# Attention's weight tiles: the scale step on ScalarE, the sign step on GpSimd, two VectorE steps in place of three

## The chip, the cores and the metric

One core of a Trainium2 chip. The metric is device time in microseconds of one execution, as the median of the runs shown. One further execution was profiled; the trace is of that one. The engines are TensorE (PE), VectorE (DVE), ScalarE (ACT), GpSimd (POOL) and SyncE (SP, which here only issues DMAs).

## The reference

```
attention: B=4, H=8, S=576, D=64; scores = q k^T / 8 - slope_h * |i - j|, kept for 0 <= i - j < 128
           attn = softmax(scores); x = attn v, heads joined to d_model = 512
block 1:   x + relu(layer_norm(x) * g @ w_ch1) @ w_ch2                  (512 -> 2048 -> 512)
block 2:   h = relu(x @ w_in); h * sigmoid(conv3(h)) @ w_out            (512 -> 1024 -> 512)
```

All inputs and the output are 32-bit floats in the reference. The kernel is handed the weights as 64-bit floats, and it makes 32-bit ones of them itself: it views a weight as two 32-bit integers, a low word and a high word. The high word, read as a 32-bit float and multiplied by 2^-112, has its exponent moved to the right place; shifted left by three it makes room for the three top bits of the low word, which are or-ed in; the sign bit has to be put back.

## The kernel before, in words

**Attention** runs first. 72 query tiles of 128 positions (9 tiles for two batches, 4 pairs of heads, 2 such blocks) are taken in 18 groups of four, counted here from 0; group g has n = 4g, and its halves are a = n and b = n + 2. The loop (lines 859 to 916) is a software pipeline, and each engine works strictly in the order in which its instructions are written. In one pass, in this order: `scores` on TensorE (line 737); the last two exponentials of the former group on ScalarE (762); `copy_turned`, ScalarE's copies of transposed q and k (838), which the scores read; `copy_p` on ScalarE (789) and `select_p` on GpSimd (796) of an older half; `join` and `minima` on VectorE (748, 752); `shares` of the former half b, on VectorE and GpSimd (770 to 774); **`extras(n, 0)`**; `values` on TensorE (812); `exponentials(a)` on ScalarE, four instructions, and two of b; `shares(a)`; `turn_p`, `copy_p` and `select_p` of the former group's a; `turn_qk` on TensorE (711) for the next group; `copy_turned`; `turn_p` of the former b; issues of loads of q, k and v on SyncE; and **`extras(n, 1)`**. The buffers of raw q, k and v are few, so SyncE waits in them for TensorE.

**Weight tiles within attention.** Twelve of the 32 weight tiles of block 1 (512 KB raw each) are loaded and converted by `extras`, one step of `weights_step` at a time. A tile that starts at key s (FINE_START, all odd) has its load issued by SyncE in the second extras of group (s - 1)/2; its six stages (FINE, line 395) are taken at s + 3 to s + 8, where an even number is the first extras of a group and an odd one the second. So the stages are, in order: `rescale` on GpSimd (line 358), first extras of group (s + 3)/2; step 0 on VectorE (shift and mask, 373), second extras; step 1 (sign from the raw high word, 378), first extras; step 2 (bits of the low word, 383), second extras; `high` on ScalarE (412), first extras; `low` on VectorE (415), second extras. The keys are 1, 3, 5, 9, 11, 13, 17, 19, 21, 23, 25, 27: groups 2, 3, 4, 6, 7, 8, 10, 11, 12, 13, 14 and 15 begin one. The raw ring has three slots.

Other extras are a layer norm's statistics and subtraction (`LN_ATT`) and the convolution's weights (`small_inputs`, whose transpose on TensorE is line 695).

**Behind attention** all work is put into a plan (class Plan): each operation has an engine, an estimated duration, and its reads and writes. `schedule` plays it through, picks for each engine the operation with the earliest due time, and so sets the order in which instructions are written. Its clock starts at 0 with the first of these operations. DMAs count with a rate and a landing time, and may not start before `late`. In block 1 each of the other 20 tiles goes through `convert_next` (line 1223): load, signs on GpSimd (364), scale on ScalarE (356), two VectorE steps (1064, 383), ScalarE's high part (996) and GpSimd's subtraction for the low part (1236). Its raw tiles are two in `xnb` and three in `fa`; the last three of these are attention's as well. `mid` results lie in one PSUM bank or in the second part of `xnb`. TensorE's products (1035) then wait for these tiles; line 1011 on VectorE makes the low part of the hidden values.

Of the kernel before, what the change touches and what calls it, by code (L numbers as in the profile page):

```python
# [14 lines left out]
ALU = mybir.AluOpType  # L15
PSUM = bass.MemoryType.PSUM

P = 128
# [17 lines left out]
class Plan:  # L36
# [58 lines left out]
    def schedule(self, pe, goal, succ, cost, rate, landing, wait):  # L95
        ops = self.ops
        n = len(ops)
        horizon = max(goal.values()) + 1e5
        due = [0.0] * n
        for i in range(n - 1, -1, -1):  # L100
            if ops[i]["eng"] == "T":
                due[i] = goal[i]
            else:
                late = min((due[j] for j in succ[i]), default=horizon)
                due[i] = late - cost(ops[i]) - self.LAT
        left = [len(op["deps"]) for op in ops]
        ready = {}
        est = [op["late"] for op in ops]
        end = [0.0] * n
        free = {}  # L110
        lock = 0.0
        dma = 0.0
        pe_at = 0

        def put(i):
            ready.setdefault(ops[i]["eng"], []).append(i)

        for i in range(n):
            if not left[i]:
                put(i)  # L120
        order = []
        starts = [0.0] * n
        stall = []
        while len(order) < n:
            best = None
            for eng, items in ready.items():
                if not items:
                    continue
                if eng == "T":
                    i = pe[pe_at]  # L130
                    if left[i]:
                        continue
                    start = max(free.get(eng, 0.0), est[i])
                else:
                    at = {i: max(est[i], dma - 3000) if ops[i]["nbytes"] else est[i] for i in items}
                    when = max(free.get(eng, 0.0), min(at.values()))
                    soon = [i for i in items if at[i] <= when + wait]
                    i = min(soon, key=lambda i: (due[i], i))
                    if at[i] > when:
                        now = [j for j in items if at[j] <= when]  # L140
                        j = min(now, key=lambda j: (due[j], j))
                        if when + ops[j]["ns"] <= at[i] + wait or due[i] > when + ops[j]["ns"] + 1500:
                            i = j
                    start = max(when, at[i])
                if ops[i]["lock"]:
                    start = max(start, lock)
                if ops[i]["nbytes"]:
                    start = max(start, dma - 3000)
                if best is None or start < best[0]:
                    best = (start, eng, i)  # L150
            start, eng, i = best
            op = ops[i]
            ready[eng].remove(i)
            if eng == "T":
                if start > free.get(eng, 0.0) + 1:
                    stall.append((free.get(eng, 0.0), start, i))
                pe_at += 1
            free[eng] = start + op["ns"]
            end[i] = start + op["ns"]
            if op["lock"]:  # L160
                lock = end[i]
            if op["nbytes"]:
                dma = max(dma, start) + op["nbytes"] / rate / 1000
                end[i] = dma + landing
            order.append(i)
            starts[i] = start
            for j in succ[i]:
                est[j] = max(est[j], end[i] + (0 if ops[j]["eng"] == eng == "T" else self.LAT))
                left[j] -= 1
                if not left[j]:  # L170
                    put(j)
        self.due = due
        return order, stall, free, starts, max(starts[i] + ops[i]["ns"] for i in pe)
# [37 lines left out]
def tile_kernel(  # L211
# [28 lines left out]
    V, S, G, T = nc.vector, nc.scalar, nc.gpsimd, nc.tensor  # L240
# [87 lines left out]
    cvn = [0]  # L328
# [63 lines left out]

    FINE = (("rescale",), (0,), (1,), (2,), ("high",), ("low",))

    def weights_step(stages, start=True, only=None):

        now = [ld for ld in reversed(flight) if only in (None, ld["only"])]
        now = [(ld, ld["stages"].pop(0)) for ld in now]  # L400
        for j in range(max((len(do) for _, do in now), default=0)):
            for ld, do in now:
                if j >= len(do):
                    continue
                kind, i, raw = ld["kind"], ld["i"], ld["raw"]
                if do[j] == "rescale":
                    t = ld["t"] = fav(FA_CV0 + cvn[0] % 3 * 512, 512).bitcast(I32)
                    cvn[0] += 1
                    rescale(t, raw, G)
                elif do[j] == "high":  # L410
                    w = wtile(kind, i)
                    S.activation(w[:, 0, :], ld["t"].bitcast(F32), AF.Copy)
                elif do[j] == "low":
                    w = wtile(kind, i)
                    V.tensor_tensor(
                        out=w[:, 1, :], in0=ld["t"].bitcast(F32), in1=w[:, 0, :].bitcast(F32),
                        op=ALU.subtract,
                    )
                    flight.remove(ld)
                else:  # L420
                    to_f32(ld["t"], raw, (do[j],), ld["mid"])
        if todo and start:
            kind, i, pool = todo.pop(0)
            raw = scratch["raw"][:, scratch["n"] % 3, :]
            scratch["n"] += 1
            if kind in ("w1", "win"):
                src = (w_ch1 if kind == "w1" else w_in)[:, 2 * i * P : 2 * (i + 1) * P]
                nc.sync.dma_start(
                    raw.rearrange("p (c f) -> p c f", f=2 * P),
                    src.rearrange("(c p) f -> p c f", p=P),  # L430
                )
            else:
                src = (w_ch2 if kind == "w2" else w_out)[i * P : (i + 1) * P, :]
                nc.sync.dma_start(raw, src)
            flight.append({
                "kind": kind, "i": i, "pool": pool, "t": None, "mid": None, "only": only,
                "raw": raw.rearrange("p (n two) -> p n two", two=2), "stages": list(stages),
            })

# [97 lines left out]
    with ExitStack() as actx:  # L537
# [128 lines left out]
        for kind, r in ((1, 2), (3, 4)):  # L666
# [6 lines left out]
            op0=ALU.add, op1=ALU.add,  # L673
# [166 lines left out]

        def extras(n: int, m: int):
            for args in fine_at.get(n // 2 + m, ()):
                weights_step(FINE, *args)
            for u in (n + 2 * m, n + 2 * m + 1):
                if u in SMALL_AT:
                    small_inputs(SMALL_AT.index(u))
                for stage, j in LN_ATT.get(u, ()):
                    layer_norm(0, j, stage, ps_r, "ptr")
# [168 lines left out]
    def dma(dst, src, nbytes, late_at=0):  # L1017

        plan.add("SP", 70, lambda: nc.sync.dma_start(dst, src), [src], [dst], nbytes=nbytes, late=late_at)
# [22 lines left out]
        reads = [a for it in items for a in it]  # L1042
        plan.add("T", ns * len(items), go, reads, [out])

    BF0 = 2000

    def convert(kind: str, i: int, raw, cv, mid=None, eng="V"):

        late_at = BF0 if raw is None else 0
        src = {"w1": w_ch1, "win": w_in, "w2": w_ch2, "wout": w_out}[kind]  # L1050
        if kind in ("w1", "win"):
            dma(
                raw.rearrange("p (c f) -> p c f", f=2 * P),
                src[:, 2 * i * P : 2 * (i + 1) * P].rearrange("(c p) f -> p c f", p=P), 524288,
            )
        else:
            dma(raw, src[i * P : (i + 1) * P, :], 524288)
        rp = raw.rearrange("p (n two) -> p n two", two=2)
        if mid is not None:
            plan.add("G", 702, lambda: signs(cv, rp), [raw], [cv])  # L1060
# [162 lines left out]
    def convert_next():  # L1223

        kind, f, _ = todo.pop(0)
        n = conv_n[0]
        conv_n[0] += 1
        raw = RAWS[n % len(RAWS)]
        cv = fav(FA_CV0 + (cvn[0] + n) % NCV * 512, 512).bitcast(I32)
        convert(kind, f, raw, cv, MIDS[n % len(MIDS)])  # L1230
        w = wtile(kind, f)
        cvf = cv.bitcast(F32)
        act(w[:, 0, :], cvf)
        plan.add(
            "G", 1350,
            lambda: G.tensor_tensor(
                out=w[:, 1, :], in0=cvf, in1=w[:, 0, :].bitcast(F32), op=ALU.subtract
            ),
            [cvf, w[:, 0, :]], [w[:, 1, :]], lock=True,
        )  # L1240
        if kind == "w1":
            if f >= FKEEP:
                dma(w1f[f], cvf, 262144)
# [675 lines left out]
```

## Time and profile before

| what | value |
|---|---|
| median of 3 runs | 737.68 us (733.99 to 738.47) |
| the profiled execution | 736.93 us, span 735.2 us |
| mean granted TensorE clock | 0.997 |
| busy share of the span | PE 97%, PEld 90%, DVE 72%, ACT 55%, POOL 32% |
| chain that ended last | PE 71%, DVE 12%, DMA 5%, POOL 5%, ACT 3%, issue 3% |
| attention | about 8 to 146.5 us |

The page divides the span into 40 slices of 18.4 us. TensorE's digits are 7 to 9 in the first eight, then 9 nearly throughout; VectorE's are 9 in slices 2 to 6; ScalarE's 8 in 1 to 3. A view in order of time gives start and duration of an instruction, and in brackets how long its engine had been idle before it and what ended that idleness. Times of TensorE's matmuls are modelled at their end.

### The profile page before, as it was taken

The numbers are of one execution on the slowest core, as the hardware profiler recorded it, in microseconds if no ns is written. First come the engines' busy times: TensorE is split into PE (matmuls) and PEld (weight loads), VectorE is DVE, ScalarE is ACT, GpSimd is POOL, SyncE is SP. The second block draws the span as 40 slices with busy tenths as digits, with TensorE's granted clock in tenths as the row PEclk, the third lists the DMA queues.
The fourth block names the chain that finished last, engine by engine and source line by source line (L and its number), as shares of the span: only waits on it lengthen the run. The fifth ranks groups of instructions, "written<-read, shape, count | busy, mean of one in ns | idle before, by whom it ended". The sixth has DMA issues, their size and how long they took to land.

```text
span 735.2 us, 13451 instructions
## 1 busy us (share of the span) xinstructions
PE 712.5 (97%) x4704; PEld 664.9 (90%) x4704; DVE 526.2 (72%) x1053; ACT 402.6 (55%) x1050; POOL 238.3 (32%) x408
## 2 busy tenths in 40 slices
PE   7999998899989999999999999999999999999998
PEld 6777876799989999999999999999999898998887
DVE  6799999567979726556679654568468998787731
ACT  4888877645424423333346333344377787776741
POOL 1778789759741202321220233242421000000000
PEclk9999999999999999999999999999999999999999
DMA  6777766238519926986860599996933000000011
GB/s 152 177 179 175 198 155 187 71 104 273 189 35 339 292 70 177 275 265 223 258 211 12 174 267 305 285 276 200 272 93 87 15 30 15 30 15 29 29 47 55
DMA packets 122303, 114.63 MB, mean 156 GB/s; under 512 B 63552, under 2 KB 87292, under 8 KB 122236
## 3 DMA queue, kind: packets, MB, share of 16 engines
q1 hardware_dynamic: 101020, 76.81, 34.6%
q0 software_dynamic: 20160, 36.71, 18.4%
q8 instruction: 37, 0.61, 0.3%
q10 hardware_dynamic: 1056, 0.26, 0.2%
q14 instruction: 30, 0.25, 0.1%
HBM read 80.70 MB, written 33.05 MB: 155 GB/s over the span
## 4 chain that ended last, share of the span: by engine, by line
PE 71%; DVE 12%; DMA 5%; POOL 5%; ACT 3%; issue 3%; SPq 0%; POOLq 0%; ACTq 0%; DVEq 0%
PE bank L1035 65%; DMA wind<-r 2%; PE ps L737 2%; DVE ps L748 2%; DVE pp L774 2%; DMA fa<-in_moe_w_in 1%; DVE mn L752 1%; POOL pt L796 1%; PE po L812 1%; DVE fa L383 1%; PE ptp L784 1%; POOL pp L774 1%; DVE fa L378 1%; ACT fa L996 1%; DMA xnb<-in_moe_w_ch 1%
## 5 line engine op out<-in xcount | busy, mean ns | idle before, releaser
L1035 PE MATMUL bank<-hhr,r 128*128 128x384 f32 x1152 | 214.0, 338 | 0.5 <-DVE fa L1003 0.5
L1035 PE MATMUL bank<-r,r 128*128 128x288 f32 (+1 forms) x1248 | 203.9, 314 | 1.3 <-ACT fa L996 1.1
L1035 PEld LDWEIGHTS bank<-hhr,r 128*128 128x128 f32 x1152 | 199.6, 188 | 2.5 <-DVE fa L1003 1.6
L1035 PEld LDWEIGHTS bank<-r,r 128*128 128x128 f32 x1248 | 193.9, 188 | 4.7 <-ACT fa L996 1.9
L1332 POOL DMA_DIRECT2D r<-w1d x96 | 51.9, 543 | 180.9 <-PE bank L1035 171.8
L996 ACT ACTIVATE fa<-bank 128x288 f32<-128x288 f32 (+1 forms) x112 | 49.8, 445 | 73.0 <-PE bank L1035 71.7
L1035 PE MATMUL bank<-r 128*128 128x512 f32 (+2 forms) x360 | 81.7, 372 | 0.1
L1035 PEld LDWEIGHTS bank<-r 128*128 128x128 f32 x360 | 63.6, 188 | 9.8 <-ACT r L1782 0.5
L996 ACT ACTIVATE r<-fa 128x256 fp32r<-128x256 f32 (+2 forms) x94 | 48.0, 521 | 39.0 <-DMA wind<-r 13.5
L996 ACT ACTIVATE hhr<-bank 128x384 fp32r<-128x384 f32 x46 | 22.5, 490 | 75.5 <-PE bank L1035 75.4
L1003 DVE TENSOR_TENSOR fa<-bank,fa 128x288 f32<-128x288 f32 (+1 forms) x88 | 43.6, 500 | 27.3 <-ACT fa L996 14.6
L762 ACT ACTIVATE pp<-ps,mn 128x128 f32<-128x128 f32 x144 | 51.4, 384 | 12.2 <-DVE mn L752 8.8
L774 POOL TENSOR_SCALAR pp<-pp,sm 128x128 f32<-128x128 f32 x72 | 43.6, 616 | 32.5 <-DVE sm L771 29.9
L1011 DVE SCALAR_TENSOR_TENSOR fa<-fa,cw 128x576 f32<-128x576 f32 x64 | 51.2, 813 | 1.5 <-ACT fa L996 0.7
L1003 DVE TENSOR_TENSOR r<-fa,r 128x256 fp32r<-128x256 f32 (+1 forms) x74 | 37.7, 521 | 19.3 <-ACT r L996 13.1
L1011 DVE SCALAR_TENSOR_TENSOR hhr<-bank,hhr 128x384 fp32r<-128x384 f32 x46 | 25.4, 552 | 35.2 <-ACT hhr L996 35.0
L796 POOL TENSOR_SCALAR_AFFINE_SELECT pt<-pc 128x512 f32<-128x512 f32 x72 | 46.7, 679 | 1.7 <-ACT pc L789 1.4
L737 PE MATMUL ps<-kt,qt 64*128 64x256 f32 x288 | 44.1, 400 | 2.6 <-ACT pp L762 1.7
L812 PE MATMUL po<-pt,rawv 128*64 128x128 f32 x544 | 37.9, 280 | 7.4 <-POOL pt L796 4.9
L1035 PE MATMUL bank<-r,hhr 128*128 128x512 f32 (+1 forms) x192 | 44.6, 381 | 0.0
L812 PEld LDWEIGHTS po<-pt,rawv 128*64 128x64 f32 x544 | 28.9, 136 | 16.0 <-POOL pt L796 12.6
L996 ACT ACTIVATE fa<-fa 128x576 f32<-128x576 f32 (+1 forms) x64 | 39.1, 620 | 2.7 <-DVE fa L1003 1.6
(146 smaller groups left out, 1138.0 us busy)
## 6 DMA issues: line engine op xcount, KB each, us to landing
r<-w1d POOLq DMA_DIRECT2D x96, 256.0 KB, 4.8
fa<-in_moe_w_ch SPq DMA_DIRECT2D x24, 512.0 KB, 4.8
w1d<-r SPq DMA_DIRECT2D x40, 256.0 KB, 3.5
wind<-r SPq DMA_DIRECT2D x28, 256.0 KB, 4.5
r<-wind POOLq DMA_DIRECT2D x28, 256.0 KB, 4.8
out<-h SPq DMA_DIRECT2D x17, 256.0 KB, 2.0
rawq<-in_q SPq DMA_DIRECT2D x32, 128.0 KB, 3.6
rawv<-in_v SPq DMA_DIRECT2D x32, 128.0 KB, 2.8
```

Source lines behind the costliest of these rows:

```text
L378: V.scalar_tensor_tensor(out=mid, in0=raw[..., 1], scalar=-0x80000000, in1=mid, op0=ALU.bitwise_and, op1=ALU.bitwise_or,)
L737: T.matmul(ps[:, h, u, :].rearrange("p (o j) -> p o j", o=2), lhs, rhs, start=i == 0, stop=i == 1,)
L748: V.copy_predicated(out=sc, mask=own4, data=ps[:, :, :, P:W])
L762: S.activation(pp[:, u, h, :], sc[:, h, u], AF.Exp, bias=mn[:, h, u : u + 1], scale=-1.0, accum_out=sm[:, 0, i : i + 1],)
L774: (G if i % 2 else V).tensor_scalar(out=pp[:, i, :], in0=pp[:, i, :], scalar1=sm[:, 1, i : i + 1], scalar2=1.0, op0=ALU.mult, op1=ALU.mult,)
L796: G.affine_select(out=parts[:, i], in_=pc, compare_op=ALU.is_ge, fill=0.0, base=base, pattern=[[0, 4], [sign, P]], channel_multiplier=-sign,)
L812: T.matmul(po[h * D : (h + 1) * D, u, :], rvs[bl, pr][:, t - 1 + i, h, :], pt[:, i, 2 * u + h, :], start=i == i0, stop=i == 1,)
L996: lambda: S.activation(now(out), now(src), func, **kw),
L1003: "V", tt_ns(cols(out)), lambda: V.tensor_tensor(out=out, in0=a, in1=b, op=op),
L1011: lambda: V.scalar_tensor_tensor(out=now(out), in0=now(a), scalar=sc, in1=now(b), op0=op0, op1=op1),
L1035: T.matmul(out, lhs, now(rhs), start=start and n == 0, stop=stop and n == len(items) - 1, skip_group_check=True,)
L1332: plan.add("G", 560, lambda: nc.gpsimd.dma_start(dst, src), [src], [dst], nbytes=262144)
```

## The change

In attention, ten tiles go through a new list of stages: `scale` on ScalarE into a separate `mid` (in `xnb`), `sign` on GpSimd (the high word times zero, which keeps its sign), `first` on VectorE (shift left by three and or with the sign), `last` on VectorE (low word's bits or-ed in), `high`, `low`. The tiles of the keys 17 and 19 keep the three VectorE steps, and have the scale on ScalarE in place of GpSimd. The places of the stages (s + 3 to s + 8) and of the loads stay. Behind attention, the planner may begin SyncE and DMAs at -10 us, and the first five raw loads are given start times of -10, -10, -2, -2 and -2 us; the other lines only take away arguments that were not used.

```diff
@@ schedule
-        free = {}
+        free = {"SP": -1e4}
         lock = 0.0
-        dma = 0.0
+        dma = -1e4
@@ weights_step
-    FINE = (("rescale",), (0,), (1,), (2,), ("high",), ("low",))
+    FINE = (("scale",), ("sign",), ("first",), ("last",), ("high",), ("low",))
+    FINE_S = (("scale",), (0,), (1,), (2,), ("high",), ("low",))
+    BY_STEPS = (17, 19)
...
-                if do[j] == "rescale":
+                if do[j] == "scale":
                     t = ld["t"] = fav(FA_CV0 + cvn[0] % 3 * 512, 512).bitcast(I32)
                     cvn[0] += 1
-                    rescale(t, raw, G)
+                    if ld["steps"]:
+                        rescale(t, raw, S)
+                    else:
+                        o = 2048 + cvn[0] % 2 * 512
+                        ld["mid"] = xnb[:, o : o + 512]
+                        rescale(ld["mid"], raw, S)
+                elif do[j] == "sign":
+                    signs(ld["t"], raw)
+                elif do[j] == "first":
+                    V.scalar_tensor_tensor(
+                        out=ld["mid"], in0=ld["mid"], scalar=3, in1=ld["t"],
+                        op0=ALU.logical_shift_left, op1=ALU.bitwise_or,
+                    )
+                elif do[j] == "last":
+                    to_f32(ld["t"], raw, (2,), ld["mid"])
@@ extras
-                weights_step(FINE, *args)
+                weights_step(FINE_S if FINE_START[args[1]] in BY_STEPS else FINE, *args)
@@ convert_next
-        convert(kind, f, raw, cv, MIDS[n % len(MIDS)])
+        convert(kind, f, raw, cv, MIDS[n % len(MIDS)], (-1e4, -1e4, -2e3, -2e3, -2e3)[n] if n < 5 else 0)
```

## Rows read from the trace of the kernel before

**Rows 1.** Windows: attention stage, busy us of each engine, clock, DMA.
```profile
8.00:146.50 138.50, 125.24 (x1297) 100.66 (x1296) 118.86 (x279) 108.39 (x437) 104.69 (x170) 1.00 0.66 164
```

**Rows 2.** Tile fa, 14 to 125 us: durations ns min/median/max.
```profile
L358 POOL TENSOR_SCALAR fa<-fa x12: 640/662/696, 26.0 to 119.4; 128x512 f32<-128x512 f32 x12
L373 DVE TENSOR_SCALAR fa<-fa x12: 414/513/852, 27.0 to 122.4; 128x512 int32<-128x512 int32 x12
```

**Rows 3.** Groups by line, 0 to 200 us: count, busy us, mean ns.
```profile
L356 ACT ACTIVATE xnb<-fa 128x512 f32<-128x512 f32 x7 | 4.6, 661 | 0.0
```

**Rows 4.** VectorE in order of time: start, duration, what [idle before].
```profile
106.57 0.51 DVE L373 TENSOR_SCALAR fa<-fa 128x512 int32<-128x512 int32 x1
107.00 0.68 DVE L748 COPY_PREDICATED ps<-own,ps 128x512 f32<-128x512 int32 x1
```

**Rows 5.** SyncE in order of time: four weight loads issued.
```profile
26.28 0.50 SPq L434 DMA_DIRECT2D fa<-in_moe_w_ch  x1
...
34.16 0.51 SPq L428 DMA_DIRECT2D fa<-in_moe_w_ch  x1
...
48.88 0.43 SPq L434 DMA_DIRECT2D fa<-in_moe_w_ch  x1
...
63.12 0.44 SPq L434 DMA_DIRECT2D fa<-in_moe_w_ch  x1
```

**Rows 6.** GpSimd in order of time: three steps at line 358.
```profile
53.77 0.68 POOL L358 TENSOR_SCALAR fa<-fa 128x512 f32<-128x512 f32 x1 [0.92 <-DMA fa<-in_moe_w_ch]
...
68.09 0.70 POOL L358 TENSOR_SCALAR fa<-fa 128x512 f32<-128x512 f32 x1 [1.18 <-DMA fa<-in_moe_w_ch]
...
81.27 0.67 POOL L358 TENSOR_SCALAR fa<-fa 128x512 f32<-128x512 f32 x1 [0.51 <-DMA fa<-in_moe_w_ch]
```

**Rows 7.** ScalarE in order of time, groups 3, 4, 6, 8, 10.
```profile
29.85 0.37 ACT L762 ACTIVATE pp<-ps,mn 128x128 f32<-128x128 f32 x1 [0.79 <-DVE mn L752]
...
36.32 0.37 ACT L762 ACTIVATE pp<-ps,mn 128x128 f32<-128x128 f32 x1 [0.32 <-DVE mn L752]
...
49.08 0.74 ACT L412 ACTIVATE r<-fa 128x512 fp32r<-128x512 f32 x1
50.38 0.37 ACT L762 ACTIVATE pp<-ps,mn 128x128 f32<-128x128 f32 x1 [0.57 <-DVE mn L752]
...
53.61 0.39 ACT L838 ACTIVATE kt<-ptr 128x256 f32<-128x256 f32 x1
...
63.97 0.37 ACT L762 ACTIVATE pp<-ps,mn 128x128 f32<-128x128 f32 x1 [0.28 <-DVE mn L752]
...
78.33 0.37 ACT L762 ACTIVATE pp<-ps,mn 128x128 f32<-128x128 f32 x1 [0.28 <-DVE mn L752]
```

**Rows 8.** TensorE in order of time: scores of group 7.
```profile
54.09 0.70 PE L737 MATMUL ps<-kt,qt 64*128 64x256 f32 x4
```

**Rows 9.** Waits of SyncE, 34.1 to 68 us: total, times, longest.
```profile
SPq L550 <- PE ptr L711: 2.0, 1, 2.0
SPq L550 <- PE ptp L784: 1.9, 2, 1.4
...
SPq L550 <- PE pcw L695: 0.5, 1, 0.5
```

**Rows 10.** Waits of all engines, 8 to 146 us.
```profile
ACT pp L762 <- DVE mn L752: 8.8, 11, 1.3
```

**Rows 11.** TensorE in order of time, at 204 us.
```profile
204.39 3.27 PE L1035 MATMUL bank<-xna,r 128*128 128x384 f32 x10 [2.49 <-POOL r L1236]
207.46 2.58 PE L1035 MATMUL bank<-hhr,r 128*128 128x384 f32 x12
```

**Rows 12.** Windows of TensorE, 206 to 208 us: busy, matmuls, clock, DMA.
```profile
206.00:208.00 2.00, 2.00 (x8) 0.50 0.00 0
```

**Rows 13.** VectorE in order of time, at 152 us.
```profile
151.99 0.68 DVE L383 SCALAR_TENSOR_TENSOR fa<-xnb,bank 128x512 int32<-128x512 int32 x1
```

**Rows 14.** GpSimd in order of time, at 153 us.
```profile
153.42 3.48 POOL L1236 TENSOR_TENSOR r<-fa,r 128x512 fp32r<-128x512 f32 x2 [8.68 <-ACT r L996]
```

More of the change, by code (lines that the diff above doesn't have):

```diff
@@ L435, in weights_step @@
             flight.append({
-                "kind": kind, "i": i, "pool": pool, "t": None, "mid": None, "only": only,
+                "kind": kind, "i": i, "pool": pool, "t": None, "mid": None, "only": only, "steps": stages is FINE_S,
                 "raw": raw.rearrange("p (n two) -> p n two", two=2), "stages": list(stages),
@@ L1043, in products, with convert @@
         plan.add("T", ns * len(items), go, reads, [out])
-    BF0 = 2000
-    def convert(kind: str, i: int, raw, cv, mid=None, eng="V"):
-        late_at = BF0 if raw is None else 0
+    def convert(kind: str, i: int, raw, cv, mid=None, late_at=0):
         src = {"w1": w_ch1, "win": w_in, "w2": w_ch2, "wout": w_out}[kind]
@@ L1053, in convert @@
                 raw.rearrange("p (c f) -> p c f", f=2 * P),
-                src[:, 2 * i * P : 2 * (i + 1) * P].rearrange("(c p) f -> p c f", p=P), 524288,
+                src[:, 2 * i * P : 2 * (i + 1) * P].rearrange("(c p) f -> p c f", p=P), 524288, late_at,
             )
         else:
-            dma(raw, src[i * P : (i + 1) * P, :], 524288)
+            dma(raw, src[i * P : (i + 1) * P, :], 524288, late_at)
         rp = raw.rearrange("p (n two) -> p n two", two=2)
```

## The prediction

> **What bounds the kernel now.** I read the page first, then windows by stage, then each engine in order of time. The page puts 71% of the chain that ended last on TensorE, and its slices show TensorE above 90% from about 146 us to the end. Behind attention one gap alone is longer than half a microsecond: 2.49 us at 204 us, waiting for GpSimd's line 1236, that is for a weight tile [rows 11]. Attention, 8 to 146.5 us, is different: TensorE 125, VectorE 119, ScalarE 108 and GpSimd 105 of 138.5 us busy [rows 1]. Four engines run in lock step, each in its own order, and what counts is who is held, and what stands behind him. VectorE is the closest thing to a bound: in group 13 the comparison step of a tile ends and the next group's join follows without a pause [rows 4].
>
> **Taken from VectorE.** Ten of the twelve tiles lose the step of line 373: median 0.51 us, at least 0.41 us [rows 2], so 10 x 0.51 = 5.1 us at most. It shortens the path only where VectorE goes straight on to the join: from 106.57 to 107.00, 0.43 us [rows 4]. I count that for groups 12 to 15, where nothing else below sets the pace: 4 x 0.43 = 1.7 us gained. Bounds 0 and 5.1 us. In groups 2 to 8 another engine will be last, next point.
>
> **Put on ScalarE: twelve scale steps, and the wait that comes with them.** One costs 0.66 us [rows 3], 7.9 us in all; ScalarE idles 0.8 us ahead of a group's exponentials (8.8 us in 11 places) [rows 10], which covers the work. It does not cover the wait. The scale reads the raw tile straight from its load, and stands in ScalarE's order just ahead of the group's exponentials; behind those are the copies of turned q and k, and behind these TensorE's scores of the next group: the copy begun at 53.61 lasts 0.39 us and the scores start at 54.09 [rows 7, 8], no slack. GpSimd does this step today, and reaches it later in the group: even so it waited for the load in three groups, until 53.77, 68.09 and 81.27 us [rows 6], while ScalarE began the exponentials of the same groups at 50.38, 63.97 and 78.33 us [rows 7]. A load lands 53.77 - 48.88 = 4.9 us after SyncE issues it [rows 5, 6].
>
> Walk it group by group, D being how much later ScalarE is than today. Group 3: load issued at 26.28, landed 31.2, scaled 31.8, exponentials at 29.85 today: D = 2.0 [rows 5, 7]. Then SyncE, ahead of its load for group 6, waits for TensorE's transposes (2.0 us) [rows 9], so that load slips by 2.0 as well. Group 4: 34.16 + 4.9 + 0.66 = 39.7 against 36.32 + 2.0: D = 3.4; the idle ahead of the next exponentials takes 0.8 back: 2.6. Group 6: 53.7 + 2.0 + 0.66 = 56.4 against 50.38 + 2.6: D = 6.0. SyncE now waits for TensorE's line 695 (0.5 us today) [rows 9], which is behind the held scores, so the load of 63.12 slips by 6.0 [rows 5]. Group 8: 68.0 + 6.0 + 0.66 = 74.7 against 63.97 + 6.0: D = 10.7, less 0.8. Another wait of SyncE for TensorE (the 1.4 us) [rows 9] passes the 10.7 on; group 10: 81.2 + 10.7 + 0.66 = 92.6 against 78.33 + 9.9: D = 14.3. In the next two groups 0.8 each comes back: **12.7 us lost** at the end of attention. Later loads have no wait in today's trace (the three of rows 6 are all), so I add no hold. Bounds: where SyncE follows nothing, one hold is left, that of group 8: 68.0 + 0.66 - 63.97 = 4.7 us; at the top, nothing taken back: 12.7 + 4 = 16.7 us. I take the walk, because each link has a wait of SyncE in the trace.
>
> [...]
>
> **GpSimd.** Its twelve rescales of 0.66 us [rows 2] become ten signs of the same form, 1.3 us less. The sign moves from between the two scalings of shares to behind the first pair of selections, ahead of the pair that TensorE's value products wait for. Where GpSimd runs through, the last selection ends when it did; where it idled, 0.66 us is added. Hidden in held groups; taken at 0, at worst 4 x 0.66 = 2.6 us in groups 12 to 15. Its waits for loads (three, in rows 6) go, but to ScalarE, as counted.
>
> **The planner behind attention.** SyncE's issues are the same in number. The planner now holds the first two loads for landed at its start, so VectorE should end the first tile's bits (line 383, at 151.99 today) ahead of the first rectified remainder, and GpSimd, idle for 8.68 us until 153.42 [rows 13, 14], starts its subtractions sooner. An advance of 2.49 us there closes the gap at 204, and the slow clock behind it: 2.5 + 1.5 = 4.0 us gained [rows 11]. Bounds: 4.0 gained, or as much lost, should the new order of five shared buffers open such a gap elsewhere; I take the gain, as the idle is three times the gap. What would be late next is TensorE's own work.
>
> **Sum.** The profiled execution took 736.9 us, 1.7 us of it around its span of 735.2; the median of the runs is 0.75 us higher. 736.9 + 12.7 - 1.7 - 4.0 = 743.9; with 0.75, **744.7 us**, 0.9% slower.
>
> **Rivals.**
> 1. SyncE runs ahead. While ScalarE is held, SyncE issues on and gains lead; then holds don't add, and group 8's 4.7 us is all. For: most of SyncE's time is issuing. Against: its waits for TensorE [rows 9]. 737.7 + 4.7 - 1.7 - 4.0 = 736.7 us: no change.
> 2. The other side, **no holds**: the loads land before ScalarE's queue reaches the scale. It decides at the order of issue in SyncE: a load 4.7 us earlier against the exponentials is enough everywhere. Then VectorE's step counts in more groups, 3.4 us (between 1.7 and 5.1), and the gap goes: 737.7 - 3.4 - 4.0 = 730.3 us, faster. Against it stand the three waits of rows 6, and that the load's place is not moved.
> [...]
> 4. The holds are as walked and the plan gains nothing: 744.7 + 4.0 = 748.7 us.
>
> **Chances and range.** Forecast 0.45, with its own range 740 to 749; rival 1 0.20; rival 2 0.18; rival 3 0.10; rival 4 0.07. One per cent, about what a measurement of this kernel can tell, is 7.4 us: 730.3 to 745.1. The forecast lies at the upper edge and gives half of itself to each side; rival 2 lies at the lower edge and does the same. Slower: 0.22 + 0.10 + 0.07, 0.40. Same: 0.23 + 0.20 + 0.09, 0.51 with rounding. Faster: 0.09. The range 731 to 752 leaves out most of rival 2's faster half and rival 3's worse half, and the selections' 2.6 us on top of them.
>
> **What would show it.** In the changed trace ScalarE's line 356 in groups 3, 4, 6, 8, 10 has idle time put down to the DMA of the weight load, 1.4 to 4.7 us, and attention ends 8 to 14 us later. If these idles are there but attention is not longer, the link by the q and k copies is wrong; if they shrink from group to group, rival 1. [...] A gap of TensorE near the fourteenth hidden tile refutes the planner's gain. VectorE's count loses ten instructions of line 373; if it doesn't, the change doesn't do what it says, which the diff gives no room for.

## The result and the profile after

The changed kernel takes **742.44 us** (median of 7 runs, 740.53 to 743.77) against 737.68 us (733.99 to 738.97, 7 runs of the kernel before beside it): ratio **1.0073, interval 1.0054 to 1.0093**, 4.8 us lost by the medians, 5.4 by the ratio. The profiled execution takes 742.44 us, its span is 740.7 us.

The head of the page of the changed kernel (engines, busy time, share, instructions):

```profile
span 740.7 us, 13470 instructions
PE 713.3 (96%) x4704; PEld 665.9 (90%) x4704; DVE 516.4 (70%) x1043; ACT 408.9 (55%) x1062; POOL 235.6 (32%) x406
```

VectorE has 10 instructions fewer than before (1053), ScalarE 12 more (1050), GpSimd two fewer (408): the change does what it says. VectorE's busy time fell by 9.8 us, and the kernel is slower: busy time was not what set the end. Lines of attention's helpers stand 16 higher than before (the scores' line 737 is now 753, the join's 748 is 764); lines 356 and 383 kept their numbers, GpSimd's subtraction of line 1236 is now 1249.

Where the time went is seen in two rows of TensorE and one of windows. The changed kernel, TensorE in order of time: the first product behind attention.

```profile
155.38 1.83 PE L1051 MATMUL bank<-hhr,r 128*128 128x384 f32 x9
```

Before, attention ended with this product at 146.52. It is **8.9 us later**, and from it to the end of the span there are 740.7 - 155.38 = 585.3 us instead of 735.2 - 146.52 = 588.7: 3.4 us shorter. 8.9 - 3.4 = 5.5 us, which is what the span grew. Windows of the changed kernel over attention, which answers to [rows 1]: busy us of the engines, clock, DMA share, GB/s.

```profile
8.00:155.38 147.38, 127.41 (x1288) 103.48 (x1284) 113.10 (x269) 114.22 (x447) 102.90 (x169) 0.97 0.63 154
```

No engine is fuller: VectorE is at 113 of 147 us where it was at 119 of 138.5. The stretch grew by waits. Which ones, ScalarE's new steps say (changed kernel, ScalarE in order of time; the bracket is the idle time ahead of the step and what ended it):

```profile
23.61 0.68 ACT L356 ACTIVATE xnb<-fa 128x512 f32<-128x512 f32 x1 [2.00 <-DMA fa<-in_moe_w_ch]
30.85 0.69 ACT L356 ACTIVATE xnb<-fa 128x512 f32<-128x512 f32 x1 [1.20 <-DMA fa<-in_moe_w_ch]
38.85 0.68 ACT L356 ACTIVATE xnb<-fa 128x512 f32<-128x512 f32 x1 [1.44 <-DMA fa<-in_moe_w_ch]
54.47 0.69 ACT L356 ACTIVATE xnb<-fa 128x512 f32<-128x512 f32 x1 [2.66 <-DMA fa<-in_moe_w_ch]
...
68.98 0.77 ACT L356 ACTIVATE xnb<-fa 128x512 f32<-128x512 f32 x1
86.41 0.67 ACT L356 ACTIVATE fa<-fa 128x512 f32<-128x512 f32 x1 [3.40 <-DMA fa<-in_moe_w_ch]
...
126.34 0.67 ACT L356 ACTIVATE xnb<-fa 128x512 f32<-128x512 f32 x1 [1.73 <-DMA fa<-in_moe_w_ch]
```

Six of twelve scale steps hold ScalarE for their weight load, 12.4 us in all. One hold can be followed through three engines. The load of 49.86 lets ScalarE go at 54.47; six exponentials, 55.07 to 57.03, and then the copy that TensorE waits for (line 805, at 57.12) are all late, TensorE stands for 2.35 us, and the next join, which has nothing else to wait for, comes at 60.47 (55.51 before). The changed kernel, TensorE, and then VectorE, at that place:

```profile
55.06 0.38 PE L727 MATMUL ptr<-ident,rawk 128*128 128x128 f32 x2
57.79 0.66 PE L800 MATMUL ptp<-ident,pp 128*128 128x128 f32 x4 [2.35 <-ACT pc L805]
58.38 0.77 PE L753 MATMUL ps<-kt,qt 64*128 64x256 f32 x4
...
60.22 1.07 PE L753 MATMUL ps<-kt,qt 64*128 64x256 f32 x4
```

```profile
60.47 0.70 DVE L764 COPY_PREDICATED ps<-own,ps 128x512 f32<-128x512 int32 x1 [2.24 <-PE ps L753]
```

Read the first joins of the 18 groups in both traces, and the loss grows by steps: at groups 3 to 5 by 2.5 us, at group 7 by 3.1 us (behind the hold of 54.47), at group 11 by 4.4 us (behind the hold of 86.41), and hardly between or after. (The very first join is 1.2 us sooner than before, so the joins lose 10.1 us and the stretch 8.9.) The clock fell behind the two longer holds (2.66 and 3.40 us); windows of TensorE in the changed kernel (busy, matmuls, granted clock, DMA share, GB/s):

```profile
56.00:60.00 4.00, 2.21 (x16) 0.86 0.74 205
60.00:64.00 4.00, 4.00 (x43) 0.71 0.64 141
88.00:92.00 4.00, 2.28 (x10) 0.70 0.70 157
92.00:96.00 4.00, 4.00 (x42) 0.87 0.64 161
```

Behind attention, TensorE's gap of [rows 11] is gone: up to 250 us no gap of its products has a releaser any more. What closed it is in two rows (changed kernel, VectorE and GpSimd), which answer to [rows 13, 14]:

```profile
157.90 0.68 DVE L383 SCALAR_TENSOR_TENSOR fa<-xnb,bank 128x512 int32<-128x512 int32 x1
```

```profile
159.33 1.63 POOL L1249 TENSOR_TENSOR r<-fa,r 128x512 fp32r<-128x512 f32 x1 [5.10 <-ACT r L1012]
```

Counted from the first product, line 383 ends a tile's bits 157.90 - 155.38 = 2.52 us in, where it was 151.99 - 146.52 = 5.47; GpSimd starts 3.95 us in, where it was 6.90. Both are 2.95 us sooner.

### The profile page after: what moved, and what is told of

It reads as the page before. It is cut to its first block, busy times and chain, and to the rows that moved or that the text cites. A ratio compares the mean times of both kernels' runs of the same rounds, so it can differ in the third digit from the quotient of the medians.

```text
span 740.7 us, 13470 instructions
## 1 busy us (share of the span) xinstructions
PE 713.3 (96%) x4704; PEld 665.9 (90%) x4704; DVE 516.4 (70%) x1043; ACT 408.9 (55%) x1062; POOL 235.6 (32%) x406
## 4 chain that ended last, share of the span: by engine, by line
PE 78%; DMA 6%; POOL 5%; ACT 4%; DVE 3%; SPq 2%; issue 1%; ACTq 0%; POOLq 0%; DVEq 0%
PE bank L1051 70%; DMA wind<-r 4%; POOL pt L812 3%; PE ps L753 2%; PE po L828 2%; PE ptp L800 2%; DMA fa<-in_moe_w_ch 1%; ACT pp L778 1%; POOL pp L790 1%; SPq L579 1%; PE ptr L727 1%; PE bank L1107 1%; ACT fa L1012 1%; DMA fa<-in_moe_w_in 1%; DVE fa L1019 1%
## 5 line engine op out<-in xcount | busy, mean ns | idle before, releaser
L790 POOL TENSOR_SCALAR pp<-pp,sm 128x128 f32<-128x128 f32 x72 | 41.1, 582 | 45.1 <-DVE sm L787 40.4
L753 PE MATMUL ps<-kt,qt 64*128 64x256 f32 x288 | 46.9, 420 | 2.6 <-ACT pp L778 1.7
```

The costliest lines, as they stand in the source:

```text
L753: T.matmul(ps[:, h, u, :].rearrange("p (o j) -> p o j", o=2), lhs, rhs, start=i == 0, stop=i == 1,)
L790: (G if i % 2 else V).tensor_scalar(out=pp[:, i, :], in0=pp[:, i, :], scalar1=sm[:, 1, i : i + 1], scalar2=1.0, op0=ALU.mult, op1=ALU.mult,)
```

## The experiments

Two theories stood against each other at first. **A**, the forecast's: the loss is ScalarE's wait for a weight load that stands ahead of the exponentials in its queue. **B**: it is the new place of GpSimd's sign, or the work that ScalarE got. The ratios are to runs of the kernel before on the same chip.

### The planner's edits alone, and attention's edits alone

The change falls into two parts with no line in common. The first kernel keeps attention as before and takes the planner's edits:

```
-        free = {}
+        free = {"SP": -1e4}
...
-        dma = 0.0
+        dma = -1e4
...
-        convert(kind, f, raw, cv, MIDS[n % len(MIDS)])
+        convert(kind, f, raw, cv, MIDS[n % len(MIDS)], (-1e4, -1e4, -2e3, -2e3, -2e3)[n] if n < 5 else 0)
```

> The planner's edits alone, attention as before. Theory (ScalarE's scale holds the exponentials until the weight load lands; the loss is all in attention): attention ends where it did, about 146.5 us, the gap of TensorE near 204 us is gone, total 737.7 - 4 = 733 to 735 us, ratio 0.994 to 0.997. Rival A (the loss comes from the planner's new order behind attention): slower than before, 741 us or more. Rivals B (the sign's place on GpSimd delays the selections) and C (ScalarE simply has 7.9 us more work): as the theory.

735.02 us, ratio **0.9990 (0.9976 to 1.0004)**: a smaller gain than expected. The gap is closed, and yet the time falls by 0.1%, by 0.2% at most.

The second kernel takes the other part: the new order of steps in attention, the planner as before.

> The edits in attention alone, the planner as before. Theory: attention ends about 9 us later as in the changed kernel and the gap near 204 us (then near 213 us) is back: 742.4 + 4 = 745 to 748 us, ratio 1.010 to 1.014. Rival A: no slower than before, 735 to 738 us. Rivals B and C: as the theory.

742.52 us, ratio **1.0103 (1.0074 to 1.0133)**, a ratio in the range expected, though the gap that was to bring it there came back small. The loss is in attention: the two parts together make 1.0093, the whole change 1.0073, no further apart than the intervals allow. Two of its rows are worth reading beside those above. ScalarE, same view:

```profile
54.47 0.69 ACT L356 ACTIVATE xnb<-fa 128x512 f32<-128x512 f32 x1 [0.38 <-DMA fa<-in_moe_w_ch]
...
71.74 0.66 ACT L356 ACTIVATE xnb<-fa 128x512 f32<-128x512 f32 x1 [4.07 <-DMA fa<-in_moe_w_ch]
87.20 0.76 ACT L356 ACTIVATE fa<-fa 128x512 f32<-128x512 f32 x1
```

The same code, but the long hold is in group 8 here, and groups 6 and 10 have next to none. And TensorE behind attention, with the planner of before:

```profile
212.60 2.00 PE L1051 MATMUL bank<-xna,r 128*128 128x384 f32 x10 [0.69 <-POOL r L1249]
```

The gap that was 2.49 us in the profiled execution of the kernel before is 0.69 us in this one, and the ten matmuls behind it take 2.00 us, not the 3.27 that they took before at a clock of 0.69 and then 0.50 (204 to 208 us): by that length the clock did not fall here.

### The scale alone

The kernel before, with nothing but its scale step moved from GpSimd to ScalarE, in the same stage; no sign, still three VectorE steps.

```
-                    rescale(t, raw, G)
+                    rescale(t, raw, S)
```

> The kernel before with one edit: the rescale of all twelve tiles by ScalarE in the same stage, in place of GpSimd; three VectorE steps stay, there is no sign step and no mid, the planner is as before. Theory: the same holds as in the changed kernel, idle of 1 to 3.5 us ahead of ScalarE's scale put down to the load in at least four groups, attention ends 8 to 11 us later: 746 to 749 us. Rival B: no sign step on GpSimd, so no loss: 736 to 738 us. Rival C: slower by several us, but without idle put down to the load.

744.94 us, ratio **1.0118 (1.0080 to 1.0156)**. Just under the microseconds expected, and the ratio says it: this one engine letter is enough for the whole loss, and B's first half falls: GpSimd has no sign here. Two of its six holds, ScalarE in order of time:

```profile
54.55 0.67 ACT L356 ACTIVATE fa<-fa 128x512 f32<-128x512 f32 x1 [3.37 <-DMA fa<-in_moe_w_ch]
...
87.06 0.67 ACT L356 ACTIVATE fa<-fa 128x512 f32<-128x512 f32 x1 [3.05 <-DMA fa<-in_moe_w_ch]
```

### The loads a group sooner

The whole change, the scale where it is, but each load is issued two stages sooner, into five raw buffers instead of three. It asks B's second half: is it the wait, or the work?

```
-            raw = scratch["raw"][:, scratch["n"] % 3, :]
+            raw = scratch["raw"][scratch["n"] % 5]
...
-                fine_at.setdefault(o + at, []).append((i == 0, key))
+                fine_at.setdefault(o + at - (2 if i == 0 and o > 1 else 0), []).append((i == 0, key))
```

> The changed kernel, the scale in its place at the head of ScalarE's queue, but each weight load issued about one group (some 7 us) sooner into a ring of five buffers. Theory A (the loss is the wait for the load's data): ScalarE's scale waits for nothing, TensorE's clock stays at 1.00 in attention, first product behind attention at 146 to 148 us instead of 155.4, time 732 to 736 us, ratio 0.994 to 0.999. Theory B (the loss is the scale's own 0.66 us on ScalarE, wherever its data are): still 739 or more, ratio over 1.003. Theory C (SyncE issues no sooner, since it stands behind its waits on TensorE): holds stay in part, 737 to 741.

733.65 us, ratio **0.9977 (0.9959 to 0.9995)**: theory A. ScalarE, steps two, four and seven of twelve:

```profile
28.96 0.77 ACT L356 ACTIVATE xnb<-fa 128x512 f32<-128x512 f32 x1
...
49.75 0.77 ACT L356 ACTIVATE xnb<-xnb 128x512 f32<-128x512 f32 x1
...
76.99 0.76 ACT L356 ACTIVATE fa<-fa 128x512 f32<-128x512 f32 x1
```

No bracket: the data are there. Only the first tile, whose load could not go sooner, is still waited for (1.30 us), and the first product behind attention is at 146.32. The waits cost (1.0073 - 0.9977) x 737.7 = **7.1 us**, give or take some 2 us by the two intervals. One expectation failed: the clock was not 1.00 throughout, but 0.82 and 0.75 from 116 to 124 us, in group 14 of this execution, behind a TensorE wait of 1.81 us for GpSimd's second pair of selections. A weight tile has a part in that wait: its sign (line 364) stands between the two pairs of selections, where the forecast's GpSimd term had put it. GpSimd, and then TensorE:

```profile
112.63 1.66 POOL L813 TENSOR_SCALAR_AFFINE_SELECT pt<-pc 128x512 f32<-128x512 f32 x2
114.27 0.67 POOL L364 TENSOR_SCALAR fa<-fa 128x512 f32<-128x512 f32 x1
...
115.85 1.22 POOL L813 TENSOR_SCALAR_AFFINE_SELECT pt<-pc 128x512 f32<-128x512 f32 x2
```

```profile
117.13 0.88 PE L829 MATMUL po<-pt,rawv 128*64 128x128 f32 x12 [1.81 <-POOL pt L813]
```

In the kernel before, where no step of a weight tile stands between these pairs, TensorE waited twice at this place, 0.80 and 1.27 us, and the clock stayed at 1.00.

### The two steps in the other order

GpSimd's sign comes first (it waits for the load, as its rescale did), ScalarE's scale one stage later, and all twelve tiles take two VectorE steps.

```
-    FINE = (("scale",), ("sign",), ("first",), ("last",), ("high",), ("low",))
+    FINE = (("sign",), ("scale",), ("first",), ("last",), ("high",), ("low",))
```

> The changed kernel with the first two stages exchanged, for all twelve tiles: the sign on GpSimd in the stage where the rescale was, the scale on ScalarE one stage later, behind the group's exponentials and copies. ScalarE has the same work, VectorE one step less for twelve tiles. Theory: at that place the load has landed, so no holds; attention ends at 142 to 146 us, and the planner's gain stays: 729 to 733 us, ratio 0.988 to 0.994, faster than both kernels. Rival C: ScalarE's work is the same, so 741 to 744 us as the changed kernel. Rival B: also faster, as the sign is back between the two scalings of shares; scale_only tells B from the theory.

733.63 us, ratio **0.9970 (0.9950 to 0.9990)**: the holds are gone (two of 0.24 and 0.28 us are left), but it is slower than what was expected, and from the first group's first join to the last group's attention takes 121.7 us against 121.2 with the planner alone. Twelve VectorE steps fewer bought next to nothing. A new wait had taken their place; waits of 28 to 126 us, first with the planner's edits alone, then with the swapped order (total, times, longest):

```profile
PE ps L737 <- ACT kt L838: 0.3, 1, 0.3
DVE ps L748 <- PE ps L737: 1.8, 3, 0.9
```

```profile
PE ps L748 <- ACT kt L849: 4.6, 10, 0.8
DVE ps L759 <- PE ps L748: 7.8, 15, 1.3
```

TensorE's scores now wait for ScalarE's copies of k, and VectorE's joins for the scores. ScalarE's rows show who is in the way, and TensorE's what it costs:

```profile
40.10 0.39 ACT L849 ACTIVATE kt<-ptr 128x256 f32<-128x256 f32 x1
40.36 0.68 ACT L356 ACTIVATE xnb<-fa 128x512 f32<-128x512 f32 x1
...
41.88 0.40 ACT L849 ACTIVATE kt<-ptr 128x256 f32<-128x256 f32 x1
```

```profile
42.33 0.70 PE L748 MATMUL ps<-kt,qt 64*128 64x256 f32 x4 [0.38 <-ACT kt L849]
```

### Each half of that by itself

Two kernels with a step left out: the planner's edits without VectorE's first step, and the swapped order without ScalarE's scale.

```
-    FINE = (("rescale",), (0,), (1,), (2,), ("high",), ("low",))
+    FINE = (("rescale",), (), (1,), (2,), ("high",), ("low",))
```

> The kernel before with the new planner alone, and VectorE's first step (shift and mask) left out for all 12 tiles: this part of the computation is missing. GpSimd still scales, ScalarE gets nothing more, so no hold. Theory A (VectorE sets the pace of attention's groups, as the forecast took it for groups 12 to 15): 1.7 us below the planner alone at the least (733.3 us, ratio about 0.997), up to 12 x 0.43 = 5.2 us (about 730, 0.992), and first to last join shorter by as much. Theory B (VectorE's step is covered, another engine closes the ring of waits): 734 to 736 us, ratio 0.998 to 1.001, joins unmoved within 0.5 us.

731.52 us, ratio **0.9953 (0.9936 to 0.9970)**, 0.0037 below the planner alone: twelve steps are worth 2.7 us, 0.23 us each, give or take 1.6 us in all by the two intervals. In time this is within theory A's range. The joins moved by less: 120.0 us from the first group's to the last group's, against 121.2 with the planner alone. The gain lies between the first joins of groups 12 and 16, which are 30.0 us apart here, 31.5 with the planner alone and 31.0 in the kernel before.

```
-    FINE = (("sign",), ("scale",), ("first",), ("last",), ("high",), ("low",))
+    FINE = (("sign",), (), ("first",), ("last",), ("high",), ("low",))
```

> The swapped order (sign first on GpSimd, then ScalarE's scale, two VectorE steps) with ScalarE's scale left out: this part of the computation is missing, VectorE reads the sign tile twice. Theory A (the 0.6 us scale on ScalarE, ahead of the copies of q and k, takes back what the dropped VectorE step gives): 2 to 5 us below the swapped order's 733.6, so 729 to 732 us, ratio 0.989 to 0.995. Theory B (neither ScalarE nor VectorE has the pace here): 733 to 735, ratio 0.996 to 0.999, and the stretch of the joins stays 121 to 122 us.

730.45 us, ratio **0.9945 (0.9927 to 0.9964)**: 0.0025, or 1.8 us, below the swapped order, just short of the 2 us expected. The two intervals overlap, but the traces bear it out: the scores wait for the copies of k for 0.3 us again, once, and the joins take 119.4 us, not 121.7. So the scale costs something in that place, though its loads were waited for only for 0.5 us there.

### The scale in ScalarE's idle time

The swapped order, the scale one stage later. There it stands ahead of the first exponentials, which wait for the minima anyway ([rows 10]). VectorE's two steps move with it, and stand together in the stage behind it.

```
-    FINE = (("sign",), ("scale",), ("first",), ("last",), ("high",), ("low",))
+    FINE = (("sign",), (), ("scale",), ("first", "last"), ("high",), ("low",))
```

> The swapped order, with ScalarE's scale one place later: just ahead of a group's first exponentials, where ScalarE idles 0.8 us for the minima, its load long landed; both VectorE steps one place later too. Theory A (a scale in that idle time is free): at or below the swapped order, 730 to 733 us, ratio 0.990 to 0.996. Theory B (it delays the exponentials all the same, or the two VectorE steps back to back at the group's end delay the next join): 734 to 738, ratio 0.998 to 1.005.

731.55 us (12 runs), ratio **0.9949 (0.9931 to 0.9968)**: the lowest ratio of all versions that compute everything, and below both kernels. ScalarE, one such place:

```profile
83.39 0.75 ACT L356 ACTIVATE xnb<-fa 128x512 f32<-128x512 f32 x1
84.91 0.37 ACT L773 ACTIVATE pp<-ps,mn 128x128 f32<-128x128 f32 x1 [0.77 <-DVE mn L763]
```

The scale lies in front of an idle stretch of 0.77 us, and the scores wait for copies of k 0.3 us, as without it. The ratio is within 0.0004 of the kernel that leaves the scale out: no cost that could be measured, though the intervals leave room for some 2 us. The joins agree: from group 0's first to group 14's, the two traces with the scale in this place (the other is that of the last experiment below, whose filler comes only then) take 97.3 and 96.3 us, and the kernel without it takes 96.3.

### The clock in the holds

Two kernels fill a wait of TensorE with transposes that nobody reads. The first is the whole change with 22 of them in groups 6 and 10:

```
+            for i in range(22 if n in (30, 46) else 0):
+                T.transpose(ptr[:, i // 2 % 2, i % 2 * P : (i % 2 + 1) * P], ident, ident)
```

> The changed kernel with 22 more transposes of the identity on TensorE in groups 6 and 10, into the bank that the turned q and k take right behind them: work that fills the stretch in which TensorE waits out a hold (2.35 us at 57.79 and 2.84 us at 89.72 in the changed kernel's trace, where the granted clock fell to 0.71 and 0.70). Theory A (the clock's fall is a part of what a hold costs): the clock stays at 1.00 there and 1 to 2 us come back for each of the two, 739 to 741 us, ratio 1.003 to 1.005. Theory B (the clock's fall is covered, since VectorE and ScalarE set the pace after a hold): the time stays at 741.5 to 744, ratio 1.006 to 1.010, with the clock at 1.00 or not.

743.49 us (6 runs), ratio **1.0108 (1.0077 to 1.0139)**. The clock is 1.00 in both places, and nothing came back, as theory B had it. But in the profiled execution the long hold was in group 8 again (3.94 us at 72.22), where there was no filler and the clock fell to 0.60 behind it (76 to 80 us), and TensorE paid 2.56 us for the transposes of group 6, where the hold was 0.49 us. So this is inconclusive on what a slow clock behind a hold costs: keeping the clock up with a filler at a fixed place did not pay here, since the hold did not keep its place.

The second fills group 14 of the late scale:

```
+                if n == 56:
+                    keep_busy(8, "v0")
                 values(a - 8)
+                if n == 56:
+                    keep_busy(8, "v1")
```

> The swapped order with the late scale, and two times 8 transposes of the identity on TensorE in group 14, ahead of either half of the values' products, where TensorE waits for GpSimd's selections (0.83 and 1.27 us in the trace with the late scale, followed by a clock of 0.61). Theory A: the clock stays at 1.00 there, attention's last join at about 129 us instead of 130.6, and the time is 729 to 731 us, ratio 0.991 to 0.994. Theory B (that fall is rare among executions, or the filler delays the products): 731 to 733, ratio 0.994 to 0.998.

732.93 us (12 runs), ratio **0.9968 (0.9952 to 0.9985)**. Attention did as theory A had it (clock 1.00, the last group's first join at 128.9 us, not 130.6), the time as theory B had it. In the profiled execution the stretch from the first product to the end was 734.5 - 144.83 = 589.7 us, against 731.5 - 146.46 = 585.0 with the late scale, which has the same products. So executions differ by 4 to 5 us there, whatever attention did, and this one is 3.3 us above the median of its kernel. What became of the 1.6 us won in attention is not shown.

## Why the forecast was right, and where its terms were off

The forecast, 744.7 us, came out 2.3 us high, with the sign, the mechanism and the place right. Its terms fare less evenly, and that they add up so nearly is luck, as the sum below shows.

**The holds: 12.7 us walked, 7.1 measured.** This is the term that was mis-sized. That the scale would stand at the head of ScalarE's queue waiting for its load, ahead of the exponentials, is shown three times: by the brackets, by the scale alone (1.0118) and by the loads a group sooner (0.9977). The step that failed is the walk's "so the load of 63.12 slips by 6.0", and, behind it, "passes the 10.7 on". Line 695, on which the first of these rests, is not among the waits of SyncE in the changed trace. The loads as the changed kernel issued them (SyncE in order of time), in the order of groups 6, 8 and 10, with the first q load that SyncE had to wait for ahead of each of the last two:

```profile
49.86 0.37 SPq L450 DMA_DIRECT2D fa<-in_moe_w_ch  x1
...
55.15 0.62 SPq L566 DMA_DIRECT2D rawq<-in_q  x1
...
64.70 0.38 SPq L450 DMA_DIRECT2D fa<-in_moe_w_ch  x1
...
72.37 0.60 SPq L566 DMA_DIRECT2D rawq<-in_q  x1
...
81.53 0.38 SPq L444 DMA_DIRECT2D fa<-in_moe_w_ch  x1
```

Group 6's load went 1.0 us later than in [rows 5], not 2.0, and group 8's went **1.6 us later, not 6.0**. The reason is in TensorE's row at 55.06: the transposes for which SyncE waited (1.2 us) are ahead of TensorE's own gap of 2.35 us, not behind the held scores as the walk had it. SyncE was released at 55.15 and issued without a pause to 64.70. So group 8's load had 4.3 us, from 64.70 to 68.98, and its scale waited for nothing. SyncE paid later: 5.0 us of waiting for TensorE up to 72.37, and group 10's scale was held instead, until 86.41, where the walk had 91.9. In the kernel with attention's edits alone it was the other way round, group 8 held and groups 6 and 10 hardly. In both traces the hold bought the next load a lead (4.3 us from issue to scale in the changed one, without a wait); that is **rival 1's** mechanism. It took part of the walk back, not all: 7.1 is between rival 1's 4.7 and the walk's 12.7. Two holds were not in the walk: group 2's of 2.00 us, and group 15's of 1.73 us, which "I add no hold" had excluded; the joins fell back by 1.3 and 0.2 us behind them. The walk's upper bound is also wrong in its own terms: 4 us are added as given back by idle time, but only the last 1.6 us of that are in the 12.7, so it should be 14.3, not 16.7.

**VectorE's step: -1.7 us forecast for ten tiles, -2.7 measured for twelve.** Taken alone it is worth 0.23 us per tile, about half of the 0.43 us between the rows of [rows 4] (whose first row is the shift and mask, which the forecast calls a comparison there): in some groups the step lies on the path, in others it doesn't. The way it was counted, four groups at full price, is borne out in place and size: without the step the joins gain 1.0 us on the kernel before, and 1.5 us on the planner alone, from group 12 to group 16, and hardly anything ahead of that. What the forecast did not see is that ScalarE's scale can take the gain back without any load being late: "which covers the work" was true of the idle time ahead of the exponentials, and not of the copies of k where the scale stands ahead of them (1.8 us in the swapped order).

**The planner: -4.0 us forecast, -0.7 measured (interval -1.8 to +0.3).** What it said of the steps came true: line 383 and GpSimd are 2.95 us sooner, more than the 2.49 us needed, and the gap is closed; so the sign that it named for this term, a gap of TensorE near the fourteenth hidden tile, could not see that it was mis-sized. The price was wrong, because it was read from one execution; that the plan gains next to nothing was rival 4's half of the truth. With the old planner the gap was 2.49 us, with a clock of 0.50 behind it [rows 12], in one profiled execution, and 0.69 and 0.67 us in two others, with the ten matmuls at 2.00 us in both; in all three line 383 comes 5.46 to 5.47 us and GpSimd 6.88 to 6.90 us behind the first product. So GpSimd's start alone did not make the gap; what made it long in that one is open. The 1.5 us for the slow clock in the 4.0 was an estimate, half of the 3.07 us between the two starts of [rows 11], and no run shows it: the ten matmuls took 1.3 us more than in the two other executions (3.27 against 2.00). And the stretch behind attention, first product to end, was 588.7, 584.5 and 587.8 us with the old planner and 584.2 to 589.7 in the nine executions with the new one: its other differences are as large as the term.

**The clock: rival 3, in part.** The granted clock did fall behind the holds, to 0.70 and 0.71 in a 4 us window. Rival 3, at 0.10, stands for such falls that lengthen the time beyond the walk; the forecast has nothing for them. TensorE's transposes did not fill the hold: they were done by 55.44 and the gap followed. But the time is 2.3 us under the forecast, not above it; the holds with their clock falls cost 7.1 us together. How much of that is clock can be estimated from rows of TensorE, the kernel before and then the changed one (the scores of group 7 stand in [rows 8] and further up):

```profile
55.30 0.70 PE L737 MATMUL ps<-kt,qt 64*128 64x256 f32 x4
...
81.82 0.66 PE L784 MATMUL ptp<-ident,pp 128*128 128x128 f32 x4
...
83.61 0.60 PE L737 MATMUL ps<-kt,qt 64*128 64x256 f32 x4
```

```profile
89.72 1.12 PE L800 MATMUL ptp<-ident,pp 128*128 128x128 f32 x4 [2.84 <-ACT pc L805]
...
92.85 0.68 PE L753 MATMUL ps<-kt,qt 64*128 64x256 f32 x4
```

From the first to the third block of scores of group 7 it is 60.22 - 58.38 = 1.84 us, and was 55.30 - 54.09 = 1.21; from the transposes behind the second hold to the second block of scores it is 92.85 - 89.72 = 3.13 us, and was 83.61 - 81.82 = 1.79. So by this estimate the slow clock made 0.6 and 1.3 us of the 3.1 and 4.4 us by which the joins fell back there. What of it is left in the time stays open.

**Rival 2, no holds**, was built: it is the kernel with the loads sooner, and its condition ("a load 4.7 us earlier is enough everywhere") holds for all tiles but the first. Priced at 7.4 us below the kernel before, it is 1.7 us below by its ratio. Two reasons are given above: a small planner term, and a VectorE step that is partly paid for on ScalarE, which was measured in the swapped order and not in this one.

**The sum with measured prices.** With the loads sooner the change is at 0.9977 and the planner alone at 0.9990, so what the VectorE steps give net of ScalarE's work is 0.0013, 1.0 us; the change divides into +7.1 (waits), -0.7 (planner) and -1.0, together 5.4 us, the ratio's 0.0073. These three close by construction, being differences of the same ratios. An independent look at the last is VectorE's -2.7 by itself and ScalarE's +1.8 in the swapped order: -0.9. The forecast's 744.7 was nearer than its terms were, since the walk (5.6 too much) and the planner (3.3 too much) erred in opposite directions. GpSimd at nothing was not tested by itself: the scale alone has no sign on GpSimd and is not faster than attention's edits (1.0118 against 1.0103), but it keeps VectorE's third step, and the two can cancel. In the traces nothing is lost there on balance: TensorE's waits for the selections come to 3.7 us in the kernel before (88 to 140 us) and to 3.7 us in the changed one (95 to 150 us).

## What to carry to other kernels

Before a step that reads straight from a load is given to another engine, look up what stands behind it in that engine's queue: the same loads were waited for on GpSimd too, for up to 1.18 us and late in the group [rows 6]; on ScalarE the waits stood ahead of the exponentials, the copies and then TensorE, and were up to 4.07 us. Let the engine with slack meet the load first, and put the moved step where its new engine already idles (in one place it cost nothing measurable, in another some 0.15 us a tile). Don't chain delays through a queue at full size: the queue that ran on while another engine was held gained lead here (group 8's load went 1.6 us later, not 6.0), so follow each wait to the instruction that ends it, and see whether that one is behind the hold or ahead of it. And a gap seen in one profiled execution is a price with one sample.

## What the runs showed of the hardware

The granted clock fell in attention with TensorE far from idle over the stretch: it was 0.61 in a 4 us window with 3.15 us busy (late scale, 116 to 120 us), behind two waits of 0.83 and 1.27 us. The length of the waits alone did not decide it in these runs. At the same place waits of 0.54 and 1.27 us (VectorE's first step left out), 0.80 and 1.27 us (the kernel before) and 1.16 and 1.27 us (the planner alone) all left it at 1.00. In the kernel of the whole change it was 0.71 and 0.70 behind waits of 2.35 and 2.84 us, and in the kernel of before 0.50 behind a single wait of 2.49 us [rows 11, 12]; but a wait of 2.40 us in group 4 of the kernel with the transposes left it at 1.00 (TensorE, and the window behind the wait):

```profile
43.12 0.66 PE L802 MATMUL ptp<-ident,pp 128*128 128x128 f32 x4 [2.40 <-ACT pc L807]
```

```profile
44.00:48.00 4.00, 4.00 (x56) 1.00 0.71 161
```

So one wait and the clock behind it, read from one trace, are no price for the next wait of that length.

The holds changed their place between executions of the same steps of attention (groups 6 and 10, or group 8), and the time hardly: 12.4 us of holds in the profiled execution of the change, 11.7 us with attention's edits alone, 12.1 us with the scale alone, at first products of 155.38, 156.54 and 156.47 us.
